# A windowed-attention and tanh-shrink kernel: the second batch moved into the first layer of chunk 0, and a table-driven interleave of the two layers

## The chip, the cores and the metric

The kernel runs on one core of a Trainium2 chip. The metric is device time in microseconds (us) of one execution, the median of the runs shown. A core has five instruction streams: TensorE (PE; its weight loads are listed apart as PEld), VectorE (DVE), ScalarE (ACT), GpSimd (POOL) and SyncE (SP). Sixteen DMA engines move data for all of them.

## The reference

The inputs are q, k and v of shape (8 batches, 8 heads, 576 positions, 64), a weight w_in (512 x 2048) and a weight w_out (2048 x 512), all float32.

```python
scores = (q @ k.T) / sqrt(64)              # per batch and head
keep   = (0 <= pos_q - pos_k) & (pos_q - pos_k < 64)
attn   = softmax(where(keep, scores, -1e9)) @ v
x   = attn.transpose(0, 2, 1, 3).reshape(4608, 512)   # tokens x (heads * 64)
h   = x @ w_in                             # first layer
out = (h - tanh(h)) @ w_out                # second layer
```

A query sees only itself and the 63 keys before it, so a block of 64 queries needs 128 keys.

## The kernel before

**Attention.** A batch is worked in four pairs of heads, numbered g = 4 * batch + pair. A pair is loaded as bf16 rows, cast or copied into a layout for PE, transposed on PE through PSUM bank 3 (`tr`, L259: six small matmuls for q, six for k, each followed by copies out of PSUM; q takes one copy on ACT and one on DVE, k one on ACT), scored (`scores`, L317: three groups of three matmuls in bank 4, an Exp on ACT after each), masked on DVE (`masking`, L325), multiplied with v (`pv`, L329, banks 5 to 7) and normalized on DVE (`norm`, L336: one reciprocal and two multiplies). When two pairs of a batch are done, their half of x is transposed into the layout of the first layer, on PE (`x_tr`, L347: two goes through PSUM, copied out by DVE or ACT) or, for later batches, with a DMA transpose (`x_dma`, L360). The first two batches use other forms of the same steps (`tr_heads` L249, `tile_scores` L284, `tile_pv` L302), with 64-wide matmuls; for pairs 1 and 2 the scores are masked by a multiply on DVE (L300), which reads a mask that lies in PSUM bank 5 (L61); for other pairs of these batches the mask is added by a matmul (`hides`, L278). The v windows `vw` are filled by small DMAs out of the cast copy `vb` (`keys_v` L173, `windows_v` L156), and in the first two batches their lower half by a DVE copy (`shift_dve`, L435).

**Layers.** The 4608 tokens are nine chunks of 512. A step of the first layer, "h, c, m" (`hp_mm`, L374), is four 128x512 matmuls into one PSUM bank, a tanh on ACT (L385), and a subtraction on DVE (`g_sub`, L388) that frees the bank and fills block m of gT. There are 16 such steps in a chunk. A step of the second layer, "y, c, st" (`yp_mm`, L399), is four 128x512 matmuls of one of four row blocks; after four steps the block is copied out by ACT and stored by SP (`y_out`, L407).

**Order.** Nothing is scheduled by a planner: `OPS` (L413) gives the layer step of each slot, `items` the attention work and the loads that are written into a slot after its layer step and before its `g_sub`. What is written is the order of each engine's stream. Slots 0 to 31 hold the 16 first-layer steps of chunk 0, one in two slots; 32 to 47 the second layer of chunk 0; 48 to 63, 64 to 79 and 80 to 95 the first layer of chunk 1, the second of chunk 1, the first of chunk 2; from slot 96 on a first-layer step of chunk c and a second-layer step of chunk c-1 alternate. The first layer of chunks 0 to 2 rotates over three banks, 0 to 2, later chunks over two (L376).

**Around the change.** Ahead of slot 0 stands batch 0 (L441 to L500). Its loads, and the loads of the weights, are all issued on POOL's queue: pair 3 after the v windows of batch 0, then both halves of w_in and of w_out, then v and the pairs of batch 1. Batch 1 is worked in slots 33 to 47, beside the second layer of chunk 0 (L502 to L534). Batches 2 and 3 begin at slots 50 and 68 (L563, L578), with casts on DVE for most pairs (L554).

The softmax here doesn't subtract the row's maximum and nothing guards it: scores larger than these inputs give would overflow.

## Time and profile before

| what | value |
|---|---|
| median of 3 runs | 349.78 us (349.37 to 354.02) |
| profiled execution, its own time | 349.35 us |
| span of its profile, first to last instruction | 347.6 us |
| PE busy | 319.6 us (92%), 2428 matmuls |
| DVE busy | 199.2 us (57%) |
| ACT busy | 184.8 us (53%) |
| POOL busy | 110.9 us (32%) |
| granted TensorE clock | 1.00 throughout |
| layer matmuls, both layers | 2 x 576 of 128x512 |
| first layer matmul starts / last matmul starts | 28.0 us / 343.4 us |

In the lines of the profile, L12 is line 12 of the kernel; a group of instructions is written as its output, an arrow, its inputs, the shapes and a count; then the busy time, the mean duration of one in ns, the idle time of its engine just before, and what ended most of that idle time. Matmuls are pipelined, so the mean duration of one (379 ns) is longer than the step from one to the next. In the table of stretches, each engine has its busy time in the stretch and, in brackets, the number of its instructions.

### The profile page before, as it was taken

How to read it: one execution, taken by the hardware profiler on the slowest of the kernel's cores; microseconds unless marked ns; L12 is line 12 of the kernel's file. 1: busy time of each engine (PE TensorE's matmuls, PEld its weight loads, DVE VectorE, ACT ScalarE, POOL GpSimd, SP SyncE). 2: the span in 40 equal slices, each digit the busy share in tenths (PEclk: the TensorE clock that was granted, in tenths of full speed). 3: DMA queues.
4: the chain of work that ended last, by engine and by line, in shares of the span. 5: the costliest groups of instructions: out<-in, count | busy, mean ns of one | idle time of the engine just before them, and what ended most of it. 6: DMA issues, size and time to landing. Idle time of an engine off the chain costs nothing.

```text
span 347.6 us, 6234 instructions
## 1 busy us (share of the span) xinstructions
PE 319.6 (92%) x2428; PEld 175.9 (51%) x2428; DVE 199.2 (57%) x328; ACT 184.8 (53%) x335; POOL 110.9 (32%) x165
## 2 busy tenths in 40 slices
PE   7578999789998777899899999999999999999995
PEld 3354545545555444555555555554555444444442
DVE  4365843667965869576766666765566444444400
ACT  3526625478645866566566666655554444444411
POOL 8821164777902722442464363510000000000000
PEclk9999999999999999999999999999999999999999
DMA  8999999589799189247598598679821300110021
GB/s 158 146 185 216 201 157 153 93 173 160 109 174 237 41 134 145 50 85 140 112 152 168 104 165 161 106 164 212 173 73 53 106 32 30 43 50 30 30 86 68
DMA packets 51494, 42.39 MB, mean 122 GB/s; under 512 B 21080, under 2 KB 44824, under 8 KB 51464
## 3 DMA queue, kind: packets, MB, share of 16 engines
q0 software_dynamic: 21536, 20.13, 38.1%
q1 hardware_dynamic: 29648, 21.50, 25.5%
q8 instruction: 19, 0.31, 0.3%
q10 hardware_dynamic: 280, 0.36, 0.3%
q14 instruction: 11, 0.09, 0.1%
HBM read 36.70 MB, written 11.21 MB: 138 GB/s over the span
## 4 chain that ended last, share of the span: by engine, by line
PE 79%; DVE 8%; ACT 5%; DMA 3%; issue 3%; POOL 1%; SPq 0%; DVEq 0%; POOLq 0%; ACTq 0%
PE ps L404 34%; PE ps L380 31%; PE ps L321 3%; PE ps L333 3%; PE ps L263 2%; DVE gT L392 2%; DMA kt<-kd 2%; DMA kall<-in_k_dram 2%; PE ps L255 2%; DVE xs L344 2%; DVE qt L85 1%; ACT th L385 1%; PE ps L293 1%; ACT pt L323 1%; DVE xs L315 1%
## 5 line engine op out<-in xcount | busy, mean ns | idle before, releaser
L380 PE MATMUL ps<-xT,wi 128*128 128x512 bf16 x576 | 144.0, 379 | 3.2 <-DVE gT L392 2.5
L392 DVE TENSOR_TENSOR gT<-ps,th 128x512 bf16<-128x512 f32 x144 | 98.6, 690 | 83.2 <-ACT th L385 81.2
L404 PE MATMUL ps<-w_out_sb,gT 128*128 128x512 bf16 x576 | 143.5, 379 | 0.0
L385 ACT ACTIVATE th<-ps 128x512 f32<-128x512 f32 x144 | 85.7, 598 | 74.0 <-PE ps L380 72.0
L380 PEld LDWEIGHTS <-wi 128*128 128x128 bf16 x576 | 61.6, 113 | 49.7 <-issue 4.1
L404 PEld LDWEIGHTS <-gT 128*128 128x128 bf16 x576 | 53.3, 98 | 54.5 <-issue 0.2
L323 ACT ACTIVATE pt<-ps 128x384 bf16<-128x384 f32 x72 | 35.3, 490 | 32.1 <-PE ps L321 31.8
L85 POOL COPY vb<-vall 72x1024 bf16<-72x1024 bf16 x24 | 24.9, 1057 | 41.6 <-DMA vall<-in_v_dram 21.3
L344 DVE TENSOR_TENSOR xs<-ps,rc 64x576 bf16<-64x576 f32 x48 | 36.2, 755 | 1.2
L409 ACT ACTIVATE ysb<-ps 128x512 f32<-128x512 f32 x36 | 21.6, 600 | 21.3 <-PE ps L404 21.3
L321 PE MATMUL ps<-qt,kt 128*128 128x128 bf16 x216 | 23.8, 219 | 2.7 <-ACT pt L323 1.4
L333 PEld LDWEIGHTS <-pt 128*128 128x128 bf16 x216 | 16.7, 98 | 14.1 <-issue 1.3
L85 DVE COPY qt<-ps 64x576 bf16<-64x576 bf16 x20 | 15.2, 760 | 13.1 <-ACT qt L83 13.1
L321 PEld LDWEIGHTS <-kt 128*128 128x128 bf16 x216 | 16.3, 98 | 12.7 <-issue 2.3
L333 PE MATMUL ps<-vw,pt 128*128 128x130 bf16 x216 | 21.4, 220 | 1.0 <-DVE xs L344 1.0
L327 DVE TENSOR_TENSOR pt<-pt,ps 128x1152 bf16<-128x1152 bf16 x24 | 17.9, 745 | 0.3 <-ACT pt L323 0.2
L296 ACT ACTIVATE pt<-ps 128x640 bf16<-128x640 f32 (+1 forms) x16 | 10.3, 650 | 11.0 <-PE ps L293 11.0
L85 POOL COPY qb<-qall 96x768 bf16<-96x768 bf16 x15 | 12.4, 830 | 10.8 <-DMA qall<-in_q_dram 10.8
L85 POOL COPY kb<-kall 96x768 bf16<-96x768 bf16 x19 | 15.8, 834 | 0.0
L85 DVE COPY kt<-ps 128x576 bf16<-128x576 bf16 x8 | 6.1, 757 | 13.8 <-PE ps L255 13.8
L96 POOL DMA_DIRECT2D qall<-in_q_dram x15 | 10.0, 668 | 12.2 <-DMA wi<-in_moe_w_in_dram 6.2
L83 ACT ACTIVATE kt<-ps 128x576 bf16<-128x576 bf16 x20 | 13.0, 648 | 1.4 <-PE ps L263 1.4
(69 smaller groups left out, 198.5 us busy)
## 6 DMA issues: line engine op xcount, KB each, us to landing
out_dram<-ysb SPq DMA_DIRECT2D x36, 256.0 KB, 2.1
vw<-vb SPq DMA_DIRECT2D x40, 130.0 KB, 4.4
vall<-in_v_dram POOLq DMA_DIRECT2D x7, 576.0 KB, 9.9
kall<-in_k_dram POOLq DMA_DIRECT2D x4, 576.0 KB, 9.2
qall<-in_q_dram POOLq DMA_DIRECT2D x4, 576.0 KB, 8.8
kall<-in_k_dram POOLq DMA_DIRECT2D x15, 144.0 KB, 5.5
qall<-in_q_dram POOLq DMA_DIRECT2D x15, 144.0 KB, 5.5
wi<-in_moe_w_in_dram POOLq DMA_DIRECT2D x2, 1024.0 KB, 13.8
```

The lines of the kernel that those rows point to most:

```text
L83: nc.scalar.activation(o, i, ACT.Copy)
L85: eng.tensor_copy(o, i)
L321: nc.tensor.matmul(sp[:, i, :], kT[g % NR][:, 64 * j:64 * j + 128], qT[g % NR][:, :, 64 * j:64 * j + 64], start=True, stop=True)
L323: nc.scalar.activation(PT[g % NPT][:, 3 * grp:3 * grp + 3, :], sp, ACT.Exp, scale=scale)
L327: nc.vector.tensor_tensor(p, p, mask.unsqueeze(1).to_broadcast([128, 2 * NJ, 64]), ALU.mult)
L333: nc.tensor.matmul(ps[:, 5 + grp, 130 * i:130 * i + 130], PT[g % NPT][:, j, :], vw[b % 2][:, j, 2 * pr:2 * pr + 2, :], start=True, stop=True)
L344: nc.vector.tensor_tensor(xo[r, :, :, pr, :], ov[r, :, :, h, 0:D], rc[r].to_broadcast([64, 3, 3, 64]), ALU.mult)
L380: nc.tensor.matmul(hp, w_in_tile(ki, m), chunk_tile(c)[:, :, ki % 2, 64 * (ki // 2):64 * (ki // 2) + 64], start=(ki == 0), stop=(ki == 3))
L385: nc.scalar.activation(th, hp, ACT.Tanh)
L392: nc.vector.tensor_tensor(gT[c][:, m, :], hp, th, ALU.subtract)
L404: nc.tensor.matmul(yp, gT[c][:, m, s * 128:(s + 1) * 128], w_out_sb[:, m, :], start=(m == 0), stop=(m == M - 1))
L409: nc.scalar.activation(ysb, ps[:, yp_bank(c, s), :], ACT.Copy)
```

## The change

The change has five parts.

1. **Loads.** Pair 3 is loaded right after pair 2. Then come the first half of w_in, v of batch 1, pairs 4 and 5, the second half of w_in, pairs 6 and 7. Both halves of w_out, v of batch 2 and pairs 8 to 11 are issued at slot 13, behind the POOL part of the v windows of batch 1. Later loads get times of their own.
2. **Batch 0.** The mask is copied from PSUM to SBUF once, and the multiply of pairs 1 and 2 reads the copy. Pair 3's transposes are moved ahead of pair 2's scores and of the first value product; all four value products follow the scores.
3. **Batch 1** is done in slots 8 to 37, most of it beside the first layer of chunk 0. Its rows are cast on DVE first, so that a transpose takes six matmuls for q and six for k in place of twelve and twelve (`tr_rows`). The first layer of chunk 0 rotates over two banks.
4. **Order of the layers.** From chunk 1 on, first-layer steps of chunk c and second-layer steps of chunk c-1 share 32 slots: AHEAD[c] second-layer steps come first, then the two alternate, then the same number of first-layer steps stands alone. AHEAD is 8, 8, 6, 4, 4 for chunks 1 to 5 and 0 after. In the tail of first-layer steps three banks are used. The second layer of chunk 0 is begun in the order of the weight halves (FIRST).
5. **Attention of batches 2 to 7** gets its slots from tables (STEPS, VALUES, LOADS). Batch 2 is cast on POOL, its v on DVE; batch 4 uses PE transposes of x in place of the DMA transpose.

```diff
+    mask_sb = const.tile([128, 64], BF16, name="mask_sb")
...
+    def copy_mask():
+        nc.vector.tensor_copy(mask_sb, mask)
...
+    def tr_rows(g, which, bank, eng):
+
+        src = rows.pop((g, which)).rearrange("p e h d -> p e (h d)")
+        tp = ps[:, bank, :].bitcast(BF16)[:, 0:E * P].rearrange("c (e p) -> c e p", e=E)
+        for e in range(E):
+            nc.tensor.transpose(tp[:, e, :], src[:, e, :], ident[:P, :P])
+        o = qs[g % 2] if which == "q" else kT[g % NR][:, 64:]
+        move(eng, o.rearrange("c (p e) -> c p e", e=E), tp.rearrange("c e p -> c p e"))
...
-            nc.vector.tensor_tensor(p, p, mask.unsqueeze(1).to_broadcast([128, 2 * n, 64]), ALU.mult)
+            nc.vector.tensor_tensor(p, p, mask_sb.unsqueeze(1).to_broadcast([128, 2 * n, 64]), ALU.mult)
...
+    AHEAD = {1: 8, 2: 8, 3: 6, 4: 4, 5: 4}
+
+    def hp_bank(c, m):
+
+        m0 = M - AHEAD.get(c, 0)
+        if m < m0:
+            return m % 2
+        a, b = m0 % 2, 1 - m0 % 2
+        return {8: (a, b, 2), 6: (a, 2, b), 4: (a, b, 2)}[M - m0][(m - m0) % 3]
...
-        outs = [ps[:, m % 3 if c < 3 else m % 2, :] for m in ms]
+        outs = [ps[:, hp_bank(c, m), :] for m in ms]
...
-        if c < 2:
-            return (1, 2)[s % 2]
+        if c == 0:
+            return (2, 1, 2, 2)[s]
         return (0, 2)[s % 2] if c == NC - 1 else 2
+
+    FIRST = (0, 1, 4, 5, 2, 3, 6, 7)
...
-        OPS[32 + m] = "y", 0, m
-        OPS[48 + m] = "h", 1, m
-        OPS[64 + m] = "y", 1, m
-        OPS[80 + m] = "h", 2, m
-        for c in range(3, NC):
-            OPS[32 * c + 2 * m] = "h", c, m
-            OPS[32 * c + 2 * m + 1] = "y", c - 1, m
         OPS[32 * NC + 2 * m + 1] = "y", NC - 1, m
+    for c in range(1, NC):
+        n = AHEAD.get(c, 0)
+        for m in range(M):
+            OPS[32 * c + (n + 2 * m if m < M - n else 16 + m)] = "h", c, m
+            st = FIRST[m] if c == 1 and m < 8 else m
+            OPS[32 * c + (m if m < n else 2 * m - n + 1)] = "y", c - 1, st
...
+    copy_mask()
     tile_scores(0, 0, (0, 1))
     tile_scores(0, 1, (4, 5))
-    for j, eng in enumerate((Y, G, A, G, Y, G, G, Y, G)):
+    for j, eng in enumerate((Y, A, G, Y, A, G, G, G, G)):
         keys_v(0, j, eng)
-    for n in "kq":
-        load(3, n, G)
     load_w_in(0)
-    load_w_in(1)
-    load_w_out(0)
-    load_w_out(1)
     load_v_all(1)
-    for g in 4, 5, 6:
+    for g in 4, 5:
         load(g, "k", G)
         load(g, "q", G)
-    load(7, "k", G)
+    load_w_in(1)
+    for g in 6, 7:
+        load(g, "k", G)
+        load(g, "q", G)
...
+    tr_heads(3, "k", 2, V)
     tile_scores(2, 0, (0, 1), "mask")
     tile_scores(2, 1, (4, 5), "mask")
-    tr_heads(3, "k", 2, V)
+    tr_heads(3, "q", 3, A)
     shift_dve(0, 0, 4)
-    tile_pv(0, (6, 7))
-    tr_heads(3, "q", 3, A)
     hides(0, (0, 1))
     hides(1, (4, 5))
     tile_scores(3, 0, (0, 1), "hidden")
     tile_scores(3, 1, (4, 5), "hidden")
-    tile_pv(1, (6, 7))
-    tile_pv(2, (2, 3))
-    tile_pv(3, (0, 1))
+    tile_pv(0, (6, 7))
+    tile_pv(1, (2, 3))
+    tile_pv(2, (0, 1))
...
+    at(9, cast_pair, 4, V)
+    at(11, cast_pair, 5, V)
+    at(12, lambda: [cast_v(1, pr, V) for pr in range(NP)])
+    at(13, lambda: [keys_v(1, j, (G, Y)[j % 2]) for j in range(NJ)])
+    at(13, load_w_out, 0)
+    at(13, load_w_out, 1)
+    at(13, load_v_all, 2)
+    for g in 8, 9, 10, 11:
+        at(13, load, g, "k", G)
+        at(13, load, g, "q", G)
+    at(19, cast_pair, 6, V)
+    at(22, cast_pair, 7, V)
+    for g, t, s0, s1 in (4, 11, 13, 14), (5, 14, 15, 15), (6, 21, 24, 25), (7, 24, 27, 28):
+        at(t, tr_rows, g, "k", 2, V)
+        at(t + 1, tr_rows, g, "q", 3, A)
+        at(s0, tile_scores, g, 0, (4, 5))
+        at(s1, tile_scores, g, 1, (6, 7) if g < 6 else (4, 5))
+    at(25, shift_dve, 1, 0, 4)
+    for pr in range(NP):
+        at(27 + 2 * pr, tile_pv, 4 + pr, (6, 7))
+    at(31, x_tr, 1, 0, 0, 4, 3, A)
+    at(32, x_tr, 1, 0, 4, 9, 4, A)
+    at(36, x_tr, 1, 1, 0, 4, 3, V)
+    at(37, x_tr, 1, 1, 4, 9, 4, A)
...
+    STEPS = {2: (39, 44, 49, 54), 3: (63, 73, 79, 84), 4: (93, 102, 108, 114), 5: (121, 127, 133, 138),
+             6: (146, 153, 160, 167), 7: (174, 182, 190, 198)}
...
+    at(36, cast_pair, 8, G)
+    at(37, cast_pair, 9, G)
+    at(40, cast_pair, 10, G)
+    at(45, cast_pair, 11, G)
...
             at(a, tr, g, "q", 3, A, V)
...
             at(a + 2, tr, g, "k", 3, A)
         for i in range(3):
             at(a + 5 + 2 * i, scores, g, i, 4)
+            at(a + 13 + i, pv, g, i)
         at(a + 11, masking, g)
-        for i in range(3):
-            at(a + 13 + i, pv, g, i)
         at(a + 15, norm, g)
-        if pr == NP - 1:
+        if b < 5:
+            if pr % 2:
+                at(a + 16, x_tr, b, pr // 2, 0, 4, 3, V)
+                at(a + 17, x_tr, b, pr // 2, 4, 9, 3, A)
+        elif pr == NP - 1:
             at(a + 16, x_dma, b)
```

More of the change, by code (lines that the diff above doesn't have):

```diff
@@ L227 @@
     nc.vector.memset(vw[0][0:64, 0], 0.0)
-    def more_constants():
-        nc.vector.memset(qT[1], 0.0)
-        nc.vector.memset(vw[1][0:64, 0], 0.0)
     def more_zeros(i):
@@ L327, in masking, with masking_sb @@
         nc.vector.tensor_tensor(p, p, mask.unsqueeze(1).to_broadcast([128, 2 * NJ, 64]), ALU.mult)
+    def masking_sb(g):
+        p = PT[g % NPT].rearrange("p j (h t) -> p (j h) t", h=2)
+        nc.vector.tensor_tensor(p, p, mask_sb.unsqueeze(1).to_broadcast([128, 2 * NJ, 64]), ALU.mult)
     def pv(g, grp):
@@ L428, in at, with flush @@
         items.setdefault(h, []).append((fn, args))
+    done = []
+    def flush():
+        if done:
+            y_out(*done.pop())
     def pace(h):
@@ L449 @@
     make_seen()
-    load(2, "k", G)
-    load(2, "q", G)
+    for g in 2, 3:
+        load(g, "k", G)
+        load(g, "q", G)
     warm(9)
@@ L460 @@
         cast_v(0, pr, V)
+    copy_mask()
     tile_scores(0, 0, (0, 1))
     tile_scores(0, 1, (4, 5))
-    for j, eng in enumerate((Y, G, A, G, Y, G, G, Y, G)):
+    for j, eng in enumerate((Y, A, G, Y, A, G, G, G, G)):
         keys_v(0, j, eng)
-    for n in "kq":
-        load(3, n, G)
     load_w_in(0)
-    load_w_in(1)
-    load_w_out(0)
-    load_w_out(1)
     load_v_all(1)
-    for g in 4, 5, 6:
+    for g in 4, 5:
         load(g, "k", G)
         load(g, "q", G)
-    load(7, "k", G)
+    load_w_in(1)
+    for g in 6, 7:
+        load(g, "k", G)
+        load(g, "q", G)
     tr_heads(1, "k", 2, V)
@@ L492 @@
     tile_scores(3, 1, (4, 5), "hidden")
-    tile_pv(1, (6, 7))
-    tile_pv(2, (2, 3))
-    tile_pv(3, (0, 1))
-    x_tr(0, 0, 0, 4, 4, A)
-    x_tr(0, 0, 4, 9, 5, A)
-    warm(2)
-    x_tr(0, 1, 0, 4, 6, V)
-    x_tr(0, 1, 4, 9, 3, A)
-    at(33, lambda: [cast_v(1, pr, V) for pr in range(NP)])
-    at(34, more_constants)
-    at(35, lambda: [keys_v(1, j, G) for j in range(NJ)])
-    at(35, load, 7, "q", G)
-    at(35, load_v_all, 2)
-    for g in 8, 9:
-        at(35, load, g, "k", G)
-        at(35, load, g, "q", G)
@@ L510 @@
-    at(39, tr_heads, 4, "k", 3, V)
-    at(40, tr_heads, 4, "q", 0, A)
-    at(41, tile_scores, 4, 0, (4, 5))
-    at(41, tr_heads, 5, "k", 3, V)
-    at(42, tile_scores, 4, 1, (4, 5))
-    at(42, tr_heads, 5, "q", 0, A)
-    at(43, tile_scores, 5, 0, (4, 5))
-    at(43, tr_heads, 6, "k", 3, V)
-    at(44, tile_scores, 5, 1, (4, 5))
-    at(44, tr_heads, 6, "q", 0, A)
-    at(45, tile_scores, 6, 0, (4, 5))
-    at(45, shift_dve, 1, 0, 4)
-    at(46, tile_scores, 6, 1, (4, 5))
-    at(46, tr_heads, 7, "k", 3, V)
@@ L524 @@
-    at(46, tr_heads, 7, "q", 0, A)
-    at(46, tile_pv, 4, (6, 7))
-    at(47, tile_scores, 7, 0, (4, 5))
-    at(47, tile_pv, 5, (6, 7))
-    at(47, tile_scores, 7, 1, (4, 5))
-    at(47, x_tr, 1, 0, 0, 4, 3, V)
-    at(47, tile_pv, 6, (6, 7))
-    at(47, x_tr, 1, 0, 4, 9, 0, A)
-    at(47, tile_pv, 7, (4, 5))
-    at(47, x_tr, 1, 1, 0, 4, 3, V)
-    at(47, x_tr, 1, 1, 4, 9, 6, A)
-    at(48, lambda: [cast_v(2, pr, G) for pr in range(NP)])
-    at(49, lambda: [windows_v(2, j, G) for j in range(NJ)])
@@ L538 @@
-    for g in 10, 11:
-        at(49, load, g, "k", G)
-        at(49, load, g, "q", G)
-    at(49, load_v_all, 3)
-    for g in range(12, 16):
-        at(60 + (g - 12) // 2, load, g, "k", G)
-        at(60 + (g - 12) // 2, load, g, "q", G)
-    for i in range(2):
-        at(140 + 4 * i, more_zeros, i)
-    def whole_pv(g):
-        for i in range(3):
-            pv(g, i)
-        norm(g)
-    def std(g, ck, cq, t, tk, ss, ms, p):
-        at(cq, cast, g, "q", V if g not in (10, 11, 15) else G)
-        at(ck, cast, g, "k", V if g not in (10, 11, 15) else G)
-        at(t, tr, g, "q", 3, A, V)
-        at(tk, tr, g, "k", 3, A)
-        for i in range(3):
-            at(ss + 2 * i, scores, g, i, 4)
-        at(ms, masking, g)
-        at(p, whole_pv, g)
@@ L563 @@
-    for i, g in enumerate(range(8, 12)):
-        a = (50, 55, 60, 65)[i]
-        lead = 3 if i < 2 else 5
-        std(g, a - lead + 1, a - lead, a, a + 2, a + 3, a + 8, a + (12 if i == 0 else 11))
-    at(70, x_tr, 2, 0, 0, 4, 3, V)
-    at(71, x_tr, 2, 0, 4, 9, 3, A)
-    at(78, x_tr, 2, 1, 0, 4, 3, V)
-    at(79, x_tr, 2, 1, 4, 9, 3, A)
-    for g in range(3 * NP, B * NP):
-        b, pr = divmod(g, NP)
-        a = 8 * g - 48 - (0, 2, 4)[min(b - 3, 2)]
-        s = 32 * b - (0, 2, 4)[min(b - 3, 2)]
-        cv, ky = s - 72 + 5 * pr, s - 54
-        if b == 3:
-            a = (68, 73, 78, 82)[pr]
-            cv = 62 + pr
-        elif b == 4:
-            a = 84 + 7 * pr
-            cv, ky = 75 + 3 * pr, 86
-        elif b == 5:
-            cv, ky = 95 + 4 * pr, 108
-        at(cv, cast_v, b, pr)
-        if b == 3:
-            lead = 3 if pr < 3 else 6
-            std(g, a - lead + 1, a - lead, a, a + 2, a + 3, a + 8, a + 11)
-            if pr == 0:
-                for j in range(NJ):
-                    at(67, windows_v, b, j, Y)
-            if pr % 2:
-                at(a + 12, x_tr, b, pr // 2, 0, 4, 3, V)
-                at(a + 13, x_tr, b, pr // 2, 4, 9, 3, A)
-            continue
-        if b < 7:
-            at(a - 7, cast, g, "q")
-            at(a, tr, g, "q", 3, A, V)
-        else:
-            at(a - 14, cast_q, g)
-            at(a - 12, bounce, g, "q")
-            at(a - 6, tr_dma, g, "q")
-        if b < 7:
-            at(a - 5, cast, g, "k")
@@ new lines, with cast_pair @@
+    tile_pv(0, (6, 7))
+    tile_pv(1, (2, 3))
+    tile_pv(2, (0, 1))
+    x_tr(0, 0, 0, 4, 6, A)
+    x_tr(0, 0, 4, 9, 7, A)
+    tile_pv(3, (4, 5))
+    warm(2)
+    x_tr(0, 1, 0, 4, 3, V)
+    x_tr(0, 1, 4, 9, 6, A)
+    def cast_pair(g, eng):
+        cast(g, "k", eng)
+        cast(g, "q", eng)
+    at(8, lambda: nc.vector.memset(vw[1][0:64, 0], 0.0))
+    at(9, cast_pair, 4, V)
+    at(11, cast_pair, 5, V)
+    at(12, lambda: [cast_v(1, pr, V) for pr in range(NP)])
+    at(13, lambda: [keys_v(1, j, (G, Y)[j % 2]) for j in range(NJ)])
@@ new lines, with behind_x @@
+    at(25, shift_dve, 1, 0, 4)
[5 more added lines that the diff above has]
+    at(37, x_tr, 1, 1, 4, 9, 4, A)
+    at(33, lambda: nc.vector.memset(qT[1], 0.0))
+    at(100, more_zeros, 0)
+    at(118, more_zeros, 1)
+    def behind_x(b):
+        last = ((b + 1) * NJ - 1)
+        nc.gpsimd.tensor_copy(tick, chunk_tile(last // WPC)[0:1, last % WPC, 0, 0:1])
@@ new lines @@
+    LOADS = {3: (50, 50, 50), 4: (73, 75, 77), 5: (98, 100, 102), 6: (130, 134, 126), 7: (145, 143, 162)}
+    STEPS = {2: (39, 44, 49, 54), 3: (63, 73, 79, 84), 4: (93, 102, 108, 114), 5: (121, 127, 133, 138),
+             6: (146, 153, 160, 167), 7: (174, 182, 190, 198)}
+    VALUES = {2: (38, 0, 42), 3: (61, 1, 65), 4: (87, 1, 91), 5: (112, 2, 120), 6: (140, 2, 152), 7: (170, 2, 178)}
+    at(36, cast_pair, 8, G)
+    at(37, cast_pair, 9, G)
+    at(40, cast_pair, 10, G)
+    at(45, cast_pair, 11, G)
@@ new lines @@
+    for g in range(2 * NP, B * NP):
+        b, pr = divmod(g, NP)
+        a = STEPS[b][pr]
+        cv, cs, ky = VALUES[b]
+        at(cv + cs * pr, cast_v, b, pr, V if b == 2 else G)
+        if b == 7:
+            at(a - 14, cast_q, g)
+            at(a - 13, cast, g, "k")
+            at(a - 12, bounce, g, "q")
+            at(a - 11, bounce, g, "k")
+            at(a - 6, tr_dma, g, "q")
+            at(a - 5, tr_dma, g, "k")
+        else:
+            if b > 2:
+                at(a - 7, cast, g, "q")
+                at(a - 5, cast, g, "k")
+            at(a, tr, g, "q", 3, A, V)
@@ L605 @@
             at(a + 2, tr, g, "k", 3, A)
-        else:
-            at(a - 13, cast, g, "k")
-            at(a - 11, bounce, g, "k")
-            at(a - 5, tr_dma, g, "k")
         for i in range(3):
             at(a + 5 + 2 * i, scores, g, i, 4)
+            at(a + 13 + i, pv, g, i)
         at(a + 11, masking, g)
-        for i in range(3):
-            at(a + 13 + i, pv, g, i)
         at(a + 15, norm, g)
-        if pr == NP - 1:
+        if b < 5:
[3 more added lines that the diff above has]
+        elif pr == NP - 1:
@@ L617 @@
             at(a + 16, x_dma, b)
-        for j in range(NJ):
-            if pr == 0:
-                at(ky + (j // 2 if b > 5 else 0), windows_v, b, j, Y)
         if pr == 0:
-            if b > 3:
-                hq, hk = s - (60 if b < 7 else 68), s - (64 if b < 7 else 72)
-                hv = {4: 69, 5: 92}.get(b, s - 78)
-                if b < 6:
-                    hk, hq = {4: (71, 72), 5: (86, 89)}[b]
-                for h, f in (hv, (load_v_all, b)), (hq, (load_all, b, "q")), (hk, (load_all, b, "k")):
+            for j in range(NJ):
+                at(ky + j // 2, windows_v, b, j, Y)
@@ L628 @@
+            if b == 2:
+                continue
+            hk, hq, hv = LOADS[b]
+            for h, f in sorted(((hq, (load_all, b, "q")), (hk, (load_all, b, "k")), (hv, (load_v_all, b))),
+                               key=lambda x: x[0]):
+                if b > 3:
                     at(h, pace, h)
-                    at(h, *f)
-    done = None
+                if (b, h) == (7, hv):
+                    at(h, behind_x, 5)
+                at(h, *f)
     for h in range(32 * NC + 32):
         op = OPS.get(h)
-        if op and done:
-            y_out(*done)
-            done = None
+        if op:
+            flush()
@@ L637 @@
         if op and op[0] == "h":
             c, m = op[1:]
-            if c < 2 and m == 0:
-                hp_mm(c, (0, 1, 2), True)
-            elif c > 1 or m > 2:
+            if c == 0 and m == 0:
+                hp_mm(c, (0, 1), True)
+            elif c > 0 or m > 1:
                 hp_mm(c, (m,), False)
@@ L645 @@
             if op[2] % 4 == 3:
-                done = op[1], op[2] // 4
+                done.append((op[1], op[2] // 4))
         for fn, args in items.pop(h, []):
@@ L650 @@
             g_sub(*op[1:])
-    y_out(*done)
+    flush()
     assert not items
```

## The prediction

> **What bounds the kernel now.** I read the busy table first, then the stretches between the layer stages (borders taken from the first matmul of each stage), then PE's and DVE's instructions in order of time, then the transfers.

> ```profile
> PE 319.6 (92%) x2428; PEld 175.9 (51%) x2428; DVE 199.2 (57%) x328; ACT 184.8 (53%) x335; POOL 110.9 (32%) x165
> PE 79%; DVE 8%; ACT 5%; DMA 3%; issue 3%; POOL 1%; SPq 0%; DVEq 0%; POOLq 0%; ACTq 0%
> ```

> The second line is the chain of waits by engine: PE holds four fifths of it. The next view gives length and busy time per stretch: start of layer 1 of chunk 0, layer 2 with batch 1, layer 1 of chunk 1, layer 2 of chunk 1, layer 1 of chunk 2, and the alternating rest.

> ```profile
> 28.02:42.54 14.52, 13.97 (x68) 7.24 (x65) 9.87 (x16) 9.56 (x17) 1.90 (x3) 1.00 1.12 209
> 42.54:69.12 26.58, 24.66 (x348) 13.55 (x346) 12.65 (x24) 10.64 (x18) 14.98 (x23) 1.00 0.84 137
> 69.12:88.42 19.30, 18.00 (x133) 10.51 (x131) 13.85 (x25) 15.37 (x30) 14.46 (x23) 1.00 1.03 167
> 88.42:111.96 23.54, 21.34 (x194) 12.70 (x191) 16.37 (x29) 12.15 (x26) 9.32 (x14) 1.00 0.95 176
> 111.96:139.95 27.99, 21.31 (x185) 13.19 (x182) 22.65 (x37) 20.09 (x40) 11.08 (x16) 1.00 0.68 108
> 139.95:347.60 207.65, 201.84 (x1231) 107.26 (x1230) 110.16 (x169) 105.94 (x189) 41.48 (x56) 1.00 0.47 100
> ```

> Columns: stretch, its us, then PE, PEld, DVE, ACT, POOL busy (count), clock, DMA share, GB/s. Busy overstates PE, so I price PE by steps from one start to the next. In order of time, PE takes 0.86 us for four layer matmuls:

> ```profile
> 147.52 1.03 PE L404 MATMUL ps<-w_out_sb,gT 128*128 128x512 bf16 x4
> 148.38 0.33 PE L321 MATMUL ps<-qt,kt 128*128 128x128 bf16 x3
> 148.55 1.02 PE L380 MATMUL ps<-xT,wi 128*128 128x512 bf16 x4
> 149.41 0.33 PE L333 MATMUL ps<-vw,pt 128*128 128x130 bf16 x3
> ```

> So a layer step is 0.864 us, three scores 0.17, three value products 0.17; likewise six transposes 0.26 and one half of `x_tr` 0.5. A pair is 2*0.26 + 3*0.17 + 3*0.17 = 1.52. Priced so, PE's work in the six stretches is 13.8, 24.3, 17.2, 20.4, 19.9, 204.1 (3.8 of the last is the store at the end), and what is left over is **0.7, 2.3, 2.1, 3.1, 8.1, 3.5: 20 us of stalls after 28.0**. The fifth stretch, layer 1 alone with dense attention, is the worst, and its DVE is 81% busy (22.65 of 27.99). Ahead of that, batch 0 takes 28.0 us:

> ```profile
> 14.10 0.37 PE L293 MATMUL ps<-qs,kt 64*128 64x64 bf16 x7 [1.29 <-DVE pt L300]
> 17.65 0.37 PE L293 MATMUL ps<-qs,kt 64*128 64x64 bf16 x7 [1.29 <-DVE pt L300]
> 20.55 0.43 PE L309 MATMUL ps<-vw,pt 128*64 128x65 bf16 x8 [1.68 <-DVE vw L181]
> 27.51 0.68 PE L350 MATMUL ps<-ident,xs 128*128 128x128 bf16 x9 [0.86 <-DVE xs L315]
> 28.02 2.75 PE L380 MATMUL ps<-xT,wi 128*128 128x512 bf16 x12
> ```

> The brackets are PE's idle time and who ended it: the mask multiply twice, the shift of v, the normalization.

> [...] the second scores of pairs 1 and 2 go to bank 5, and each waits 1.29 us for a multiply whose only tie to them is the mask in that bank. [...] w_out halves issued at 15.7 and 16.4 land 20.0 and 24.2 us later, behind w_in.

> **Part by part. Start (loads, mask copy, pair 3).** The mask copy takes the two waits of 1.29 out of the chain; pair 3's transposes then lie before pair 2's scores, so the shift is bound by the v windows. These are issued by 12.9 as before (`cast_v` ends at 9.76); pair 3's two loads now precede them, 288 KB. The 64 x 2080 shift is 1.31 in all; in its place 19.8 I put 18.5, first product at 19.9, four normalizations of 1.04 (0.22 + 0.82) to 25.2, x_tr and copies to 26.0. The first half of w_in landed at 14.2 + 11.7 = 25.9 and has the same bytes ahead of it, so nothing before 25.9 is to be had. **First layer step at 26.0: minus 2.0.** The copy itself is one 128x64 DVE instruction; the nearest row is the 128x128 memset, 0.17, beside PE's work; at most 0.2.

> **Chunk 0's first layer with batch 1.** What changes most. A step's bank comes free after matmuls, tanh, subtraction:

> ```profile
> 31.32 1.02 PE L380 MATMUL ps<-xT,wi 128*128 128x512 bf16 x4 [0.55 <-DVE gT L392]
> 32.38 0.60 ACT L385 ACTIVATE th<-ps 128x512 f32<-128x512 f32 x1 [0.86 <-PE ps L380]
> 33.01 0.69 DVE L392 TENSOR_TENSOR gT<-ps,th 128x512 bf16<-128x512 f32 x1 [0.55 <-ACT th L385]
> ```

> 31.32 to 33.70 is 2.4 us. With three banks that is 0.8 per step, under 0.864; with two it is 1.2, so a bare step loses 0.34. Steps 0 to 5 have no attention beside them: 2.1 lost. Then ten steps share PE with batch 1. PE's work up to slot 32: 16*0.864 = 13.8, transposes 8*0.26 = 2.1 (before: 8*0.38 = 3.0), scores 4*1.15 = 4.6, three value products 1.3, a part of x_tr 0.3: 22.1. DVE in that time: 16 subtractions at 0.66 = 10.6, casts 8*0.35 = 2.8, cast of v 1.4, four copies of k 3.0, shift 1.3, three normalizations 3.1, memset 0.5: 22.7. Neither is full, but the handoffs are tight: cast, transpose, copy, scores, Exp come one behind the other on the in-order queues, with one layer step between where before there was a second-layer step free of DVE. Bound of what is lost: none beyond the 2.1, as the rest of PE's work could fill it; at most one 1.2 us handoff for each of the ten later steps, 12, and 14 with the first. I take 8: **slot 32 at 26.0 + 22.1 + 8 = 56.1.** Eight second-layer steps (6.9) with batch 1's rest (1.2) and 0.5 of waits end at 64.7. Before, the same work (chunk 0's first layer, batch 1, half of the second) stood at 69.1 - 6.9 = 62.2. So **this part is 2.5 behind, after a start 2.0 ahead**: it costs 4.5.

> The loads: v, pairs 4 and 5 (1152 KB) come between the halves of w_in. At the 4.9 us per 1024 KB at which weight halves landed, pair 4 is there by about 31, the second w_in by 38, pair 7 by 41. Pair 4 is cast at about 33, w_in's second half is needed at 41: both hidden; with the cover gone, each us late is a us lost, since DVE and PE stand in order. w_out is issued behind POOL's v windows at slot 13, about 42 to 44, and lands at about 52 and 57, for slots 32 (56) and 36 (60). SP is passed by four of the v windows; it holds nothing else then.

> **After slot 40.** Left are 264 layer steps, 228.1; batches 2 to 4 with x_tr, 12*1.52 + 3*1.0 = 21.2; 5 and 6, 12.2; 7 (DMA transposes), 4.0; the end, 3.8. 64.7 + 269.3 = **334.0 plus stalls**. In that region the kernel before has 2.1 + 3.1 + 8.1 + 3.5 = 16.8 of them. What replaces them:
> - `norm` (0.22 + 1.52) and its x_tr are now one slot apart, six times. DVE takes 1.74 plus a handoff, PE has one step, 0.86, and a score: 0.8 each, 4.8. (Batch 4's x_tr, 1.0, is in the work.)
> - Three times the first layer of a chunk follows x_tr's ACT copies: 0.4 each, 1.2.
> - Second-layer steps in a row have one bank (2) for chunks 1 on: an ACT copy of 0.60 and handoffs at slots 68 and 100, 1.0.
> - Five tails of layer 1 alone (8, 8, 6, 4, 4 steps). For eight steps with 1.6 pairs: DVE 8*0.66 + 1.6*3.2 = 10.4 (a pair is 0.76 + 0.75 + 1.74 = 3.2) against PE's 6.9 + 2.4 = 9.3; short enough for three banks to soften. 1.5.
> - Late rest, mainly the DMA-transposed batch 7: it had 3.5; 1.5.
> Sum 10.0, bounds 3 and 17 (the old total). POOL's casts for batch 2 are 4*1.66, beside PE. **Span 344.0**; with 1.75 around it (349.35 - 347.6) 345.8, against the profiled 349.35: 1.0% less. The median shown is 0.4 higher, so **346**.

> **Rivals.** (1) Alternation is as smooth as in 140 to 160 of the old trace, where PE shows 9.97 of 10: stalls of 3 after slot 40 and 5 in layer 1 of chunk 0 give 334.0 - 3 + 3 + 1.75 + 0.4 = **336**. For: DVE is 53% busy in the old alternation. Against: three tails, six tight x_tr. (2) The stalls move, not vanish: 11 in chunk 0, 14 after: 334.0 + 3 + 14 + 2.15 = **353**. For: handoffs of two banks. (3) The other side: transfers. Behind slot 13's issue come v windows (585 KB), w_out (2048), v of batch 2 (576) and pair 8 (288): 3.5 MB. At the 209 GB/s of 28 to 42 they are there 17 us after 43, at 60; at the whole span's mean, 122, after 29, at 72, and POOL's cast adds 1.7. The slot 39 transposes are due at about 63: 11 late, with everything behind them, **357**. It decides below about 125 GB/s. Against: the queue ran faster whenever it was full.

> **Chances.** Forecast 0.42, rival 1 0.26, rival 2 0.17, rival 3 0.15. Two per cent, about what a measurement of this kernel can tell from no change, is 343 to 357. Faster: rival 1 and a little of the forecast, 0.28; slower: rival 3 and a third of rival 2, 0.20; same 0.52. Range 336 to 357: half of rival 1 and half of rival 3 lie outside. The forecast's own range, with both signs about it, is 341 to 350.

> **What would show it.** First L380 matmul near 26.0, no bank-5 wait; slot 32 near 56 (rival 1: 53, rival 2: 59); DVE or ACT as releaser there. Waits of x_tr for L344 of about 0.8, six times. Idle PE waiting for `w_out_sb` or `qall` would be rival 3. I am wrong if layer 1 of chunk 0 runs much nearer to 1.4 us per step or much over 2.

## The result, and the profile after

The changed kernel takes **376.81 us** (median of 4 runs, 376.61 to 378.01) against 349.57 for the kernel before on the same chip: 1.0754 times as long by the means, 95% interval 1.0665 to 1.0843. A run that took over 1.5% more than the fastest of its kernel is left out of the medians and ratios below (one of win6_early, one of both_3banks). The changed kernel's profiled execution took 376.61 with a span of 374.9, so 27.3 us of span came on top of the 347.6 of before.

The busy table, the granted clock and the chain of waits of the changed kernel:

```profile
PE 327.1 (87%) x2366; PEld 178.8 (48%) x2398; DVE 201.2 (54%) x332; ACT 183.9 (49%) x338; POOL 104.5 (28%) x153
PEclk9989999999999999999999996999699999999999
PE 57%; DMA 14%; DVE 12%; ACT 5%; issue 5%; POOL 4%; SPq 2%; ACTq 0%; POOLq 0%; DVEq 0%
```

PE's share of the chain fell from 79 to 57%, DMA's rose from 3 to 14%. The clock row has two deep dips, in slices 25 and 29 of the 40, and a small one in slice 3. Stretches of the changed kernel, from first layer step to slot 32, from slot 40 to 144.5, to slot 160, to slot 192, and to the end:

```profile
25.55:55.34 29.79, 24.36 (x267) 13.37 (x266) 20.62 (x40) 17.18 (x30) 10.22 (x16) 0.98 1.07 169
...
64.55:144.50 79.95, 70.95 (x534) 40.57 (x539) 48.69 (x77) 46.48 (x90) 32.02 (x44) 1.00 0.69 121
144.50:215.20 70.70, 66.12 (x506) 38.56 (x512) 47.40 (x75) 45.70 (x87) 30.58 (x41) 1.00 0.67 119
215.20:270.80 55.60, 39.74 (x233) 20.97 (x237) 25.07 (x39) 20.60 (x39) 10.32 (x16) 0.88 0.64 123
270.80:374.90 104.10, 99.16 (x483) 49.04 (x492) 40.08 (x60) 40.73 (x70) 0.00 (x0) 1.00 0.19 56
```

The kernel before, for slots 160 to 192 alone:

```profile
211.00:244.10 33.10, 32.41 (x214) 17.90 (x213) 20.77 (x34) 19.11 (x35) 9.58 (x15) 1.00 0.78 158
```

Slots 160 to 192 hold 16 steps of either layer in both kernels: 33.1 us before, **55.6 after, at a mean clock of 0.88**. The changed kernel came to slot 160 only 4.2 later (215.2 against 211.0) with about 1.2 us of attention work still owed (PE's work, estimated by the prediction's prices); it left slot 192 26.7 later (270.8 against 244.1), and the rest took 104.1 against 103.5. So some 21 of the 27 us lie in these 32 slots. PE's instructions there that waited longest, in the changed kernel:

```profile
220.27 0.22 PE L346 MATMUL ps<-vw,pt 128*128 128x130 bf16 x1 [0.58 <-DMA vw<-vb]
227.34 0.27 PE L346 MATMUL ps<-vw,pt 128*128 128x130 bf16 x1 [6.86 <-DMA vw<-vb]
227.40 1.91 PE L429 MATMUL ps<-w_out_sb,gT 128*128 128x512 bf16 x4
...
261.00 0.22 PE L346 MATMUL ps<-vw,pt 128*128 128x130 bf16 x1 [1.47 <-DMA vw<-vb]
262.30 0.22 PE L346 MATMUL ps<-vw,pt 128*128 128x130 bf16 x1 [1.08 <-DMA vw<-vb]
262.35 1.83 PE L403 MATMUL ps<-xT,wi 128*128 128x512 bf16 x4
```

The value products of batch 6, and later of batch 7, wait for their windows of v, and behind a wait four layer matmuls take 1.9 us in place of 1.03: the clock is at half from 224.9 to 231.7 and from 262.4 to 269.2. Why the windows are late stands in SP's queue (start, length):

```profile
204.18 2.51 SPq L161 DMA_DIRECT2D vw<-vb  x3
210.25 2.88 SPq L378 DMA_TRANSPOSE xT<-xs  x2
213.23 3.71 SPq L161 DMA_DIRECT2D vw<-vb  x4
...
217.70 0.77 SPq L161 DMA_DIRECT2D vw<-vb  x1
```

The windows of batch 6 are written into slots 152 to 156, the DMA transposes of x of batch 5 into slot 154, between them. From 206.7 to 210.25 SP stands at those transposes, which wait for the normalization of batch 5's last pair; five windows stand behind. The last is issued at 217.70 and its product runs at 227.34, 9.6 us later. In the kernel before, the same windows stood well ahead of the transposes:

```profile
186.91 4.00 SPq L160 DMA_DIRECT2D vw<-vb  x5
...
200.31 2.83 SPq L365 DMA_TRANSPOSE xT<-xs  x2
```

There the first window was 19 slots ahead of the first value product (134 to 153); in the changed tables it is 7 (152 to 159), and for batch 7 nine (178 to 187, before 19).

The new tables also contain a fault. They write pair 28's q transpose (slot 168) ahead of the last three score matmuls of pair 26 (slot 169), and both pairs use the same buffer. These matmuls wait for that transfer (1.81 us at 239.91) and then read pair 28's q: **for the last 192 queries of two heads of batch 6 the changed kernel does not compute the attention of the reference.** The same holds for all kernels below that leave pair 28 where the change put it; with pair 28 at 176, it is pair 28's last scores that read pair 30's q. The number of instructions is the same either way.

### The profile page after: what moved, and what is told of

It is laid out like the page before. It is cut to its first block, busy times and chain, and to the rows that moved or that the text cites. A ratio compares the mean times of both kernels' runs of the same rounds, so it can differ in the third digit from the quotient of the medians.

```text
span 374.9 us, 6143 instructions
## 1 busy us (share of the span) xinstructions
PE 327.1 (87%) x2366; PEld 178.8 (48%) x2398; DVE 201.2 (54%) x332; ACT 183.9 (49%) x338; POOL 104.5 (28%) x153
## 4 chain that ended last, share of the span: by engine, by line
PE 57%; DMA 14%; DVE 12%; ACT 5%; issue 5%; POOL 4%; SPq 2%; ACTq 0%; POOLq 0%; DVEq 0%
PE ps L429 24%; PE ps L403 24%; DMA vall<-in_v_dram 7%; DMA vw<-vb 6%; DVE xs L357 5%; DVE gT L415 3%; PE ps L346 2%; PE ps L330 2%; ACT th L408 2%; PE ps L263 2%; SPq L161 1%; PE ps L363 1%; DVE qt L86 1%; DMA qt<-qd 1%; ACT ysb L434 1%
## 5 line engine op out<-in xcount | busy, mean ns | idle before, releaser
L403 PE MATMUL ps<-xT,wi 128*128 128x512 bf16 x576 | 150.2, 386 | 4.8 <-DVE gT L415 4.1
L346 PE MATMUL ps<-vw,pt 128*128 128x130 bf16 x216 | 25.7, 221 | 16.2 <-DMA vw<-vb 13.5
L346 PEld LDWEIGHTS <-pt 128*128 128x128 bf16 x216 | 18.2, 98 | 23.8 <-issue 4.2
L330 PE MATMUL ps<-qt,kt 128*128 128x128 bf16 x216 | 24.2, 222 | 1.9 <-DMA qt<-qd 1.8
L86 POOL COPY kb<-kall 96x768 bf16<-96x768 bf16 x24 | 19.9, 829 | 17.5 <-DMA kd<-kb 10.1
L86 POOL COPY vb<-vall 72x1024 bf16<-72x1024 bf16 x20 | 20.6, 1052 | 13.8 <-DMA vall<-in_v_dram 13.8
L86 POOL COPY qb<-qall 96x768 bf16<-96x768 bf16 x20 | 16.7, 834 | 17.1 <-DMA qall<-in_q_dram 8.6
L353 DVE RECIPROCAL rc<-ps 128x9 f32<-128x9 f32 x24 | 5.2, 218 | 27.0 <-PE ps L346 26.7
L463 POOL COPY tick<-gT 1x1 bf16<-1x1 bf16 x12 | 2.1, 179 | 49.3 <-DVE gT L415 49.3
L84 ACT ACTIVATE xT<-ps 128x512 bf16<-128x512 bf16 (+4 forms) x20 | 8.6, 479 | 14.5 <-PE ps L363 14.5
```

What stands on the lines that cost most here:

```text
L84: nc.scalar.activation(o, i, ACT.Copy)
L86: eng.tensor_copy(o, i)
L330: nc.tensor.matmul(sp[:, i, :], kT[g % NR][:, 64 * j:64 * j + 128], qT[g % NR][:, :, 64 * j:64 * j + 64], start=True, stop=True)
L346: nc.tensor.matmul(ps[:, 5 + grp, 130 * i:130 * i + 130], PT[g % NPT][:, j, :], vw[b % 2][:, j, 2 * pr:2 * pr + 2, :], start=True, stop=True)
L403: nc.tensor.matmul(hp, w_in_tile(ki, m), chunk_tile(c)[:, :, ki % 2, 64 * (ki // 2):64 * (ki // 2) + 64], start=(ki == 0), stop=(ki == 3))
```

## Experiments

| kernel | median us | ratio of the means to before on the same chip [95%] |
|---|---|---|
| changed kernel | 376.81 | 1.0754 [1.0665, 1.0843] |
| win6_early | 370.11 | 1.0578 [1.0516, 1.0640] |
| win7_early | 370.83 | 1.0616 [1.0548, 1.0684] |
| both_early | 364.81 | 1.0415 [1.0341, 1.0489] |
| v7_later | 377.57 | 1.0777 [1.0712, 1.0841] |
| old_win6_late | 363.40 | 1.0352 [1.0318, 1.0386] |
| old_new_start | 348.86 | 0.9937 [0.9910, 0.9965] |
| both_3banks | 362.62 | 1.0348 [1.0300, 1.0396] |
| both_xtr_later | 362.33 | 1.0320 [1.0260, 1.0379] |
| pair28_later | 382.50 | 1.0899 [1.0856, 1.0941] |
| all_four | 380.76 | 1.0846 [1.0808, 1.0884] |
| pair28_one_later | 367.11 | 1.0445 [1.0376, 1.0513] |
| all_four_b | 362.73 | 1.0332 [1.0276, 1.0388] |
| v7_no_tick | 363.96 | 1.0415 [1.0371, 1.0460] |
| old_tuned | 347.70 | 0.9900 [0.9868, 0.9933] |

The theory: v windows that stand too late or behind a transpose in SP's queue cost the 21 us. Rivals: the transfers themselves are slow (v of batch 7 loaded beside them), or the handoffs of the interleave (banks, transposes of x).

**Windows of batch 6, of batch 7, and both, earlier.** A triple is the slot of the first cast of v, the slots from one cast to the next, and the slot of the first window; for batch 7 the casts move too.

```diff
-            6: (140, 2, 152), 7: (170, 2, 178)
+            6: (140, 2, 148), 7: (170, 2, 178)      win6_early
+            6: (140, 2, 152), 7: (166, 1, 170)      win7_early
+            6: (140, 2, 148), 7: (166, 1, 170)      both_early
```

> One number of the changed kernel is altered: the window copies of batch 6 stand at slots 148 to 152 instead of 152 to 156, so all nine are ahead of the DMA transpose of x of batch 5 (slot 154) on SP. Theory queue order (the last five windows stand on SP behind that transpose, which waits for a normalization, so they land when the value products of pair 24 already wait): the waits for vw between 217 and 227 (9.3 us) go, and with them the stretch of half clock behind (6.8 us at half, 3.4 lost): 376.8 - 12.5 = 364. Theory sharing (the last window was slow because the load of v of batch 7 ran beside it): much the same, since these windows now come before that load. Theory interleave (handoffs between the engines cost the time, the windows only show where PE would have waited anyway): over 372.

> Batch 7 alone: its v is cast at slots 166 to 169 and its windows stand at 170 to 174, instead of 170 to 176 and 178 to 182. Theory queue order: the waits for vw between 259 and 265 (4.1 us) go, and the half clock behind them (6.8 us, 3.4 lost): 376.8 - 7.5 = 369; the wait at 227 stays. Theory interleave: within 2 us of 376.8.

> Both of these edits. Theory queue order: the two gains add up, 376.8 - 20 = 357, and what is left over the kernel before, 7 us, is the stalls between slots 40 and 160 that the prediction had at half their size. Theory interleave: over 370.

6.7 less, 6.0 less, and both together 12.0 less: within the spread of the runs the two add. In both_early no product of batches 6 and 7 waits for a window. So the place of the windows, with the casts of batch 7 that feed them, is shown to cost 12 us, and not the 20 that were expected: batch 6's edit gave 6 us less than expected, the pair 8 less, as other stops came up behind. The waits for transfers that PE has left in slots 160 to 192 of both_early:

```profile
233.41 0.34 PE L330 MATMUL ps<-qt,kt 128*128 128x128 bf16 x3 [2.83 <-DMA qt<-qd]
254.65 0.34 PE L330 MATMUL ps<-qt,kt 128*128 128x128 bf16 x3 [1.03 <-DMA kt<-kd]
```

**The load of v of batch 7 out of the way of the windows.** Windows as in the change.

```diff
-    7: (145, 143, 162)
+    7: (145, 143, 166)
```

> The load of v of batch 7 is issued at slot 166 instead of 162, behind a wait for the first layer step of slot 164, so that it does not run beside batch 6's last window, which in the changed kernel was issued at 217.7 and landed by 227.3. Theory sharing: that window lands in the usual 4.4 us, the wait of 6.9 shrinks to about 2, the clock stays up: 376.8 - 8 = 369. Theory queue order: its lateness is that of its issue behind the transposes and their own transfers; gain under 2 us, or a loss of a few us where batch 7's v now comes later.

377.57, no gain. PE's waits in v7_later:

```profile
224.15 0.22 PE L346 MATMUL ps<-vw,pt 128*128 128x130 bf16 x1 [1.50 <-DMA vw<-vb]
...
238.92 0.50 PE L330 MATMUL ps<-qt,kt 128*128 128x128 bf16 x3 [6.12 <-DMA qt<-qd]
```

The last window, issued at 219.24, now served its product after 4.9 us in place of 9.6. But the load, moved to 229.5 to 238.0, now lies beside pair 28's q transpose: issued at 230.68, it serves the scores after 8.2 us, where the changed kernel has 3.9 (235.98 to 239.91). So the delay moves with the load: in these two runs the small transfer beside the 576 KB was the slow one. The load is issued by POOL, the slowed transfers by SP, and that did not keep them clear of each other (9.6 us against 4.9, 8.2 against 3.9). The theory had the wait of batch 6 as a matter of the queue alone, which was wrong; the rival had a gain of 8, which was wrong too. Early windows take the wait away in either case.

**The same late windows made in the kernel before.** Its batch 6 windows moved to slots 146 to 150, around its transposes of x in slot 148; nothing else.

```diff
             cv, ky = 95 + 4 * pr, 108
+        elif b == 6:
+            ky = 146
```

> The kernel before with batch 6's window copies at slots 146 to 150 instead of 134 to 138: the DMA transpose of x of batch 5 (slot 148) falls among them and the value products of pair 24 (slot 153) follow 7 slots after the first, as in the changed kernel. Theory queue order: the changed kernel's stop comes back in the old one, 5 to 7 us of waiting for vw and a stretch of half clock: 349.6 + 10 = 360. Theory interleave: no more than 2 us.

363.40, which is 13.0 more. Two of the value products' waits on PE in old_win6_late:

```profile
214.40 0.27 PE L333 MATMUL ps<-vw,pt 128*128 128x130 bf16 x1 [3.69 <-DMA vw<-vb]
218.14 0.44 PE L333 MATMUL ps<-vw,pt 128*128 128x130 bf16 x2 [3.47 <-DMA vw<-vb]
```

Behind them four layer matmuls took 1.91 (at 218.70) where they had taken 1.02 (at 209.68), and those from 220.89 took 1.07 again. So late windows around a transpose of x do it by themselves, without any other part of the change.

**The new start in the kernel before** (mask copy, order of pair 3 and the products, pair 3's loads first, the engines that issue the v windows, the banks of x's transposes; the cut shows part of it).

```diff
+    copy_mask()
     tile_scores(0, 0, (0, 1))
...
+    tr_heads(3, "k", 2, V)
     tile_scores(2, 0, (0, 1), "mask")
     tile_scores(2, 1, (4, 5), "mask")
-    tr_heads(3, "k", 2, V)
```

> The kernel before with the start of the changed one alone: mask copied to SBUF, pair 3 loaded and transposed early, the four value products after the scores, the engines of the v windows. The prediction's term for this part, minus 2.0: first layer step at 26.0 instead of 28.0, 347.6 in all. The trace of the changed kernel has that step at 25.55, minus 2.4. Theory clock (the rearranged start has idle stretches in which the clock falls to half): the gain is partly lost, 348 to 350.

348.86 against 350.41. Its first layer step is at 25.20 in place of 28.02, the second chunk at 67.6 in place of 69.1, the third at 111.9 against 112.0. The start is worth 2.8 where it is made and nothing 84 us later, in the profiles; POOL's casts of batch 2 begin at 80.46 in this kernel as in the one before, waiting for q. The median gain of 1.5 lies in the interval that the ratio gives, 1.2 to 3.2.

**Three banks for chunk 0's first layer; the transposes of x one slot later.** Each on top of both_early. The third bank is taken from batch 1's k transposes, which then share bank 3 with those of q.

```diff
         m0 = M - AHEAD.get(c, 0)
+        if c == 0:
+            return m % 3                                       both_3banks
...
-        at(t, tr_rows, g, "k", 2, V)
+        at(t, tr_rows, g, "k", 3, V)                           both_3banks
...
-                at(a + 16, x_tr, b, pr // 2, 0, 4, 3, V)
-                at(a + 17, x_tr, b, pr // 2, 4, 9, 3, A)
+                late = 1 if pr == 1 else 0                     both_xtr_later
+                at(a + 16 + late, x_tr, b, pr // 2, 0, 4, 3, V)
+                at(a + 17 + late, x_tr, b, pr // 2, 4, 9, 3, A)
```

> The changed kernel with batches 6 and 7 early, and chunk 0's first layer on three banks (0, 1, 2) instead of two, for which batch 1's k transposes go to bank 3 like the q ones. Against the run with both early (364.8). Prediction's term for the two banks (1.2 us per bare step instead of 0.864): the six first steps give back 2.1, the later ones up to 4 less what the shared bank 3 costs: 360 to 363. If the handoffs of batch 1 alone set that stage: within 1 us.

> The changed kernel with batches 6 and 7 early, and the transposes of the first half of x of batches 2, 3 and 4 one slot later (61, 90, 119 instead of 60, 89, 118 for their first go). Each waits 1.0 us for its normalization in the traces; with one layer step (0.86) more in between three waits of 1.0 go: 364.8 - 2.6 = 362.2. If PE only waits for the next thing instead (bank 3, the step after): within 1 us.

362.62 and 362.33, by the ratios 0.6 and 0.9% under both_early, with intervals that overlap: the times can't tell either from nothing. The third bank shows no gain in the traces either. From the first layer step to slot 32 it takes 32.3 us (25.37 to 57.65), both_early with two banks 32.4 (25.95 to 58.37), the changed kernel with two banks 29.8. The waits between the first bare steps are gone, but q's transposes now wait for k's copy out of bank 3 (0.77, 0.92 and 0.24). That fits the other expectation, that the handoffs of batch 1 set this stage. Of the three waits of x_tr meant, near 95, 131 and 169, the first fell from 1.01 to 0.73 (start to start) and the others are gone, as expected.

**Pair 28, two slots later and one slot later.**

```diff
-    7: (174, 182, 190, 198)
+    7: (176, 182, 190, 198)        pair28_later, all_four
+    7: (175, 182, 190, 198)        pair28_one_later, all_four_b
```

> The run with both early, and pair 28 starts two slots later (176 instead of 174). In the changed kernel the DMA transpose of pair 28's q stands at slot 168, one slot ahead of the third group of scores of pair 26 (slot 169), in the buffer that both share: that group is put behind this transfer, and takes pair 28's q for these three blocks; with the edit it comes first, and takes pair 26's. In the traces PE waits there for the transfer, 1.8 us (changed kernel), 2.8 (both early), 6.1 (v of batch 7 later), with half clock behind it. Theory slot tables (each transfer that the tables put too close costs its own stop): this wait and its half clock go, 364.8 - 4 = 361. If something else of batch 7 comes late just as much: within 1 us.

> All edits of the changed kernel together: batches 6 and 7 early, pair 28 later, x_tr of the first halves later, three banks in chunk 0. Theory slot tables: the gains add, 364.8 - 4 - 2.5 - 1 = 357. What then stands over the kernel before (7 us) is its later arrival at slot 40 (2.3) and the handoffs that are left between slots 40 and 160. Theory interleave (a stop removed is only replaced by the next): over 361.

> The changed kernel with both windows of batches 6 and 7 early (364.8), and pair 28 one slot later (175 for 174): its q transpose is then written behind the last scores of pair 26 in slot 169, its k transpose in slot 170 ahead of the windows of batch 7, and its last scores in slot 184 ahead of pair 30's q transpose; each group of scores reads its own pair's q. Theory (the stop at 233 comes from the order of two instructions on one buffer): no wait of a score group for a q transfer is left near 233, and with the half clock behind it some 4 us go: 361. Rival (the transfers of batch 7 are late whatever the order, as the two later forms of this edit showed): another wait for kt or qt of batch 7 takes the place, 364 or more.

> The same, with the transposes of x of the odd pair 1 of batches 2 to 4 one slot later, and three banks for the first layer of chunk 0. Theory (the stops are separate, so their prices add): 364.8 less 4 (pair 28) less 2.5 (transposes of x) less 1 (banks) is 357, still above the kernel before by about 7, which then is the price of the handoffs of the interleave itself in slots 40 to 160. Rival (the stops hide each other, so that what one leaves the next takes): 361 or more.

Two slots later: 382.50, a miss by 21. In pair28_later the stop was moved and not taken away: k of pair 28 now stood behind the windows of batch 7, and its last scores behind pair 30's q transpose, which stood in SP's queue behind the transposes of x of batch 6:

```profile
247.82 0.43 PE L330 MATMUL ps<-qt,kt 128*128 128x128 bf16 x3 [4.85 <-DMA kt<-kd]
266.45 0.50 PE L330 MATMUL ps<-qt,kt 128*128 128x128 bf16 x3 [12.82 <-DMA qt<-qd]
```

all_four missed for the same reason (14.8 us for pair 30's q). One slot later each group stands ahead of the transfer that overwrites its q, so these kernels read the right q. With it all_four_b takes 362.73 where all_four took 380.76: **18 us for one slot of one pair**, and nothing else differs. But against both_early the one slot gains nothing (1.0445 against 1.0415): the wait at 233 is gone, and pair 29 waits for its k. PE's wait in pair28_one_later:

```profile
253.21 0.50 PE L330 MATMUL ps<-qt,kt 128*128 128x128 bf16 x3 [4.53 <-DMA kt<-kd]
```

SP's queue in pair28_one_later, from batch 7's first window to the k transpose that is waited for:

```profile
237.05 0.66 SPq L176 DMA_DIRECT2D vw<-vb  x1
...
250.44 1.27 SPq L142 DMA_TRANSPOSE kt<-kd  x1
```

PE comes to these scores at 248.7, in both_early at 253.6 (254.65 less its wait of 1.03), so it is 4.9 ahead; the k transpose is only 1.2 ahead (250.44 against 251.59). What one stop leaves, the next takes; the rival was right. That the prices add, which had held for the two window edits, doesn't hold here.

**Batch 7's v without its hold.** all_four_b, with the load no longer behind the transposes of x of batch 5.

```diff
-    7: (145, 143, 162)
+    7: (145, 143, 156)
...
-                if (b, h) == (7, hv):
-                    at(h, behind_x, 5)
```

> all_four_b with the load of batch 7's v at slot 156 and without its wait for the transposes of x of batch 5. In all_four_b that load is issued at 218.5, right behind the transposes that end at 217.97, lands at 226.6, and POOL stands 7.3 us for it with the casts of pairs 29 to 31 behind; SP then has the windows of batch 7 at 232 to 243 and pair 29's k transpose behind them, for which the scores wait 4.3. Theory (the rest behind slot 160 is one chain from the transposes of x, over POOL's cast of v, to SP's windows and transposes): the chain starts some 6 us earlier, the waits of 4.3 and 2.3 and the half clock go, 8 in all: 355. Rival (the load and the transposes of x then share the transfers and each comes later; or SP's windows are the limit by themselves): within 2 of all_four_b, 361 or more.

363.96, no gain. v is issued 4.6 earlier (213.92 against 218.50), but POOL's cast of it starts only 2.5 earlier (224.13 against 226.64), and the transposes that run at the same time take 7.44. SP's queue in all_four_b:

```profile
211.14 4.59 SPq L378 DMA_TRANSPOSE xT<-xs  x2
```

SP's queue in v7_no_tick:

```profile
213.58 7.44 SPq L378 DMA_TRANSPOSE xT<-xs  x2
```

And what PE waits for there, in v7_no_tick:

```profile
224.04 1.02 PE L405 MATMUL ps<-xT,wi 128*128 128x512 bf16 x4 [1.93 <-DMA xT<-xs]
```

The wait for pair 29's k fell to 0.72, and one for x of 1.93 came. Issued side by side, the load and the transposes each took longer (10.2 us from issue to cast against 8.1, and 7.44 against 4.59), so the rival held.

**The start and later transposes of x in the kernel before.** old_new_start, with x_tr of batches 2 and 3 one and two slots later.

```diff
-    at(70, x_tr, 2, 0, 0, 4, 3, V)
-    at(71, x_tr, 2, 0, 4, 9, 3, A)
+    at(71, x_tr, 2, 0, 0, 4, 3, V)
+    at(72, x_tr, 2, 0, 4, 9, 3, A)
...
+                late = 2 if pr == 1 else 0
+                at(a + 12 + late, x_tr, b, pr // 2, 0, 4, 3, V)
+                at(a + 13 + late, x_tr, b, pr // 2, 4, 9, 3, A)
```

> The kernel before with the new start, and three of its x_tr moved off the slots of other users of bank 3: 71 and 72 instead of 70 and 71 for batch 2's first half, 87 and 88 instead of 85 and 86 for batch 3's. In the trace of before the waits around bank 3 there are 0.7 (97.5), 0.9 (121.5) and 1.2 (125.2). If they are the limit: 348.9 - 2.5 = 346.4. If DVE is (22.65 of 28 us busy in that stretch): 348.9 within 1 us.

347.70 (345.59 to 348.26, 6 runs) against 350.81: 1.0% less, interval 0.7 to 1.3. That is small, but it is under the kernel before and far under the changed one. The start is the one part of the change that is shown to help, by 0.6%.

## Why the prediction was wrong, step by step

Its path up to slot 40 held, and its region after slot 40 didn't. Times after are of the profiled execution; waits are from the start of one PE instruction to the next, less PE's work by the prediction's prices. So the 7.7 are 55.34 less 25.55 less its 22.1 of work, and the 41 are 374.9 less 64.55 less its 269.3.

| step | predicted | measured |
|---|---|---|
| first layer step | 26.0 | 25.55 |
| stalls in chunk 0's first layer | 8 | 7.7 |
| slot 32 | 56.1 | 55.34 |
| slot 40 | 64.7 | 64.55 |
| norm to x_tr | 4.8 | 5.6 |
| first layer after x_tr | 1.2 | 0.4 |
| one bank of the second layer | 1.0 | 1.4 |
| tails of layer 1 alone | 1.5 | 2.2 |
| waits not on the list | 0 | some 7 |
| late rest | 1.5 | some 23 |
| all stalls after slot 40 | 10.0 | 41 |

**Start.** Right, to 0.5 us; in eleven more profiles with this start the first layer step is at 25.4 to 27.0. The two waits of 1.29 for the mask are gone, and each second score goes in one piece (18 matmuls), in the changed kernel:

```profile
15.69 0.66 PE L302 MATMUL ps<-qs,kt 64*128 64x64 bf16 x18 [0.51 <-ACT qs L84]
...
25.55 2.56 PE L403 MATMUL ps<-xT,wi 128*128 128x512 bf16 x8
```

The scores take columns 0 to 319 of bank 5 and the mask 448 to 479, so what tied the two together before was the bank and no address: with the copy in SBUF these scores wait for no multiply, where two had waited 1.29 each.

**Batch 1 beside chunk 0, and the loads.** Right to 1 us, and in part by luck: in seven more profiles of kernels that are alike up to slot 60, slot 32 stands at 54.7 to 59.3. In four of them a value product waits 1.4 to 2.3 us for the shift of v, behind a late window; in the changed kernel's it waits 0.3. No second-layer matmul waits for w_out, so rival 3 didn't occur; pair 8's cast held PE by 0.54. By its own sum (3.5 MB from 43 on, then a cast of 1.7, due at 63) lateness sets in below some 190 GB/s, and 125 would be 10 us late; the trace has 184 GB/s from 43 to 61, and the half microsecond fits that. Rival 3 did have the right kind of cause, late transfers, in the wrong place.

**Handoffs.** Four of the five terms came out at 9.6 in sum against 8.5. Missing on the list were waits of a value product for the mask, 3.1 in three places: with pairs five slots apart the normalization of the pair before stands one slot ahead of the mask on DVE. Windows of batch 2 gave 1.7, k transposes behind q's copies 1.9, the cast 0.5. The changed kernel, one wait of each kind, the priced and the missed:

```profile
91.30 0.40 PE L363 MATMUL ps<-ident,xs 128*128 128x128 bf16 x4 [0.84 <-DVE xs L357]
...
100.46 0.34 PE L346 MATMUL ps<-vw,pt 128*128 128x130 bf16 x3 [1.04 <-DVE pt L336]
```

**The step that failed: "Late rest, mainly the DMA-transposed batch 7: it had 3.5; 1.5".** Batches 5 to 7 were priced by PE's work, with 1.5 for all their stalls, and no term of the forecast was for a slower clock. The new tables move windows, bounces through DRAM and DMA transposes of these batches past each other on SP, and that queue was walked for batch 1 alone ("it holds nothing else then"). In slots 160 to 192 PE's work is 33.4 us (32 layer steps of 0.864; 84 matmuls of scores and values at a third of 0.17; 24 transposes at a sixth of 0.26), so 22.2 of the 55.6 are stall. The brackets of PE's waits sum to 15.7; PE worked at half clock for 4.4 and some 6 us, half of which, about 5, is lost; the rest is small gaps. Of the 22.2, 12 are shown by experiment to hang on the place of the v windows, half clock included. The remainder, some 10, lies by the traces in batch 7's chain of load, cast, windows and transposes, whose parts trade places when one is moved; no run takes it away. The upper bound of 17, "the old total", was no bound: it came from a kernel with 19 slots between a window and its product.

**What stays open.** all_four_b is still 12.0 above the kernel before on its chip. In its profile about 9 us of stall lie in slots 160 to 192 (waits of 4.45, 2.32 and 0.67 from start to start, and half of 3.4 us at half clock), where the kernel before has 0.9; that leaves some 4 for all else, mainly ahead of slot 160. No run separates these two by edits.

## What to carry to other kernels

When a change reorders tables of slots, walk every in-order queue, the DMA-issuing one too, and for each small transfer note the slots from issue to use and what stands ahead of it that waits for compute: here windows around one transpose, 7 and 9 slots ahead of their use in place of 19, cost 12 us, more than the four handoff terms together (9.6). Look up where each buffer is rewritten as well; one slot of one pair was worth 18 us, and one slot too early it gave wrong scores. A stall priced from a profile is a price for that place only: two window edits added up, later ones uncovered the next stop.
